# Forward borders of a linear-attention and GLU training step: new order with residuals on TensorE, and backward weights transposed by DMA

## The chip, the cores and the metric

The kernel runs on one core of a Trainium2 chip. The metric is device time in microseconds for one execution. The kernel before takes 1199.76 us (median of three runs, 1198.84 to 1200.74).

## The reference

Four residual layers are computed forward, attention, feed-forward, attention, feed-forward, and then the gradients of all inputs. S = 2048 rows, D = 512, F = 1376, 32 heads of 16. Cut to what matters:

```python
def attention(x, wqkv, wo):                 # linear attention, H = 32, Dh = 16
    q, k, v = split_heads(x @ wqkv)
    phi = lambda t: where(t > 0, t + 1, exp(t)) + 1e-6
    pq, pk = phi(q), phi(k)
    kv = einsum("bhsd,bhse->bhde", pk, v)
    z = einsum("bhsd->bhd", pk)
    num = einsum("bhqd,bhde->bhqe", pq, kv)
    den = einsum("bhqd,bhd->bhq", pq, z)[..., None] + 1e-6
    return merge_heads(num / den) @ wo

def feed_forward(x, w_gate, w_up, w_down):
    return (sigmoid(x @ w_gate) * (x @ w_up)) @ w_down

x = x + attention(layernorm(x), wqkv, wo)
x = x + feed_forward(layernorm(x), w_gate, w_up, w_down)
x = x + attention(layernorm(x), wqkv, wo)
x = x + feed_forward(layernorm(x), w_gate, w_up, w_down)
# outputs: x, and the gradients for grad_out of x, wqkv, wo, w_gate, w_up, w_down
```

Both attention layers share their weights, and so do both feed-forward layers. Inputs and outputs are bf16.

## The kernel before

The 2048 rows are cut into 16 row tiles of 128 (`NST`), D into four chunks of 128 (`NDC`), F into eleven (`NFC`, the last of 96). The residual stream stays in SBUF as f32 tiles `k.xs`. The forward part runs as `kq_fwd` (layer 0), `ab_fwd` (layer 1), `kq_fwd` (layer 2), `ab_fwd` (layer 3); what the gradients need is stored to DRAM tensors (`sv_...`) and read again in the backward part, which follows.

`kq_fwd` does attention as far as it can go without all rows. For each row tile it computes phi of k and q, and adds h^T phi(k) into four PSUM banks (`X_some`, L612); `z_sum` adds phi(k) up on GpSimd. After the loop comes the border to the feed-forward: the last terms of z (L735, L738), the last X matmuls and X copies (L748 to L750), `kv_ps` (L758), its block-diagonal part `kvbdT` (L760), M = kvbdT times wo in four matmuls and copies (L763 to L766), the queries of the last two row tiles (`late_q`), and MT, which only the backward part reads (L772 to L783).

A row tile of attention output then goes through the steps of `attn_fronts`: `prod` (phi(q) times z), `front1` (sum per head, `den`), `front2` (1/den, and `pqn`), `front3` (transpose of pqn, `pqnT`), `attn_mm` (four matmuls with M, L854), `attn_add` (residual added on VectorE from PSUM, L862, then LayerNorm statistics, L448). LayerNorm goes on with three GpSimd steps (L451 to L454), `apply` on ScalarE (L459) and `stage_T`, the transpose that gives hT (L494, copied by VectorE).

`ab_fwd` loops over the row tiles. `gu` makes gate and up matmuls for each of three slices of F, two sigmoids on ScalarE (L911, L913), hh on VectorE (L914) and ssd on GpSimd (L915). `transposes` makes hhT (L923, copied by ScalarE, L926). `finish` is the down-projection of the row tile before (L935) and its residual. Between them stand the attention steps of row tiles ahead: `attn_y(st + 2)`, `front1` to `front3` of `st + 3`, `apply(st + 2)`, `stage_T(st + 1)`. At a row tile's end ssd, hdd and hdl are stored. `ssd_t`, `hh_t` and `hhT` have two buffers each. The tables of ScalarE change with the functions: one line loads that for Sigmoid ahead of the feed-forward (L771).

Weights in transposed form, for the gradients, are made on TensorE: `wT_groups_a` (wqkv and wo, in layer 1) and `wT_groups_b` (w_down, w_up, w_gate, in layer 3) give groups of up to four 128x128 transposes in one PSUM bank with one evacuation. The class `Fill` hands them out in `A.tail` and at places in the loop of `ab_fwd`, `fill("t", ...)`, so that they are spread over the row tiles.

TensorE, ScalarE, VectorE and GpSimd run their instructions in the order in which the program issues them (`tc.manual_schedule`). The order on SP, which issues all DMAs, is set by the scheduler. PSUM is divided into pools by name: "t" two banks, "g" two, "u" two, "y" one, "ln" one.

Of the kernel before, what the change touches and what calls it, by code (L numbers as in the profile page):

```python
# [10 lines left out]
F32 = mybir.dt.float32  # L11
# [31 lines left out]


def pair_cols(fc):
    if fc == NFC - 1:
        return slice(fc * P, F)
    c0 = fc // 2 * 2 * P + fc % 2
    return slice(c0, c0 + 2 * P - 1, 2)
# [18 lines left out]
def kernel(  # L68
# [78 lines left out]
    with tc.tile_pool(name="wfwd", bufs=1, reuse_waits="tile") as wfwd, ExitStack() as lctx, tc.manual_schedule(engines=EM):  # L147
# [44 lines left out]
        with tc.tile_pool(name="aq0", bufs=1, reuse_waits="tile") as aq:  # L192
            A = kq_fwd(k, aq, 0, lns[0], lns[1], x_bf)
            with tc.tile_pool(name="wt_stage", bufs=2, reuse_waits="tile") as wt_stage:
                fill = Fill(wT_groups_a(k, wt_stage))
                A.tail(fill)
                ab_fwd(k, A, lns[1], fill, nxt=lns[2])
        xctx.close()
        with tc.tile_pool(name="aq2", bufs=1, reuse_waits="tile") as aq:
            A = kq_fwd(k, aq, 2, lns[2], lns[3])  # L200
            hctx.close()
            wb = bctx.enter_context(tc.tile_pool(name="wbwd", bufs=1, side="right", reuse_waits="tile"))
            ocur = {}
# [27 lines left out]
            fill = Fill(wT_groups_b(k, wb))  # L231
            A.tail(fill)
            ab_fwd(k, A, lns[3], fill, out_cb=out_cb, last_cb=last_cb)
# [5 lines left out]
    if True:  # L239
        def load_b_weights():  # L240
            k.wdT = wb.tile([P, NDC, F], BF16, name="wdT", tag="w_c")
            nc.sync.dma_start(out=k.wdT[:], in_=k.wT["wdT"].rearrange("(c p) f -> p c f", p=P))
            k.wuT = wb.tile([P, NFC, D], BF16, name="wuT", tag="w_a")
            k.wgT = wb.tile([P, NFC, D], BF16, name="wgT", tag="w_b")
            for t_sb, t_d in ((k.wuT, k.wT["wuT"]), (k.wgT, k.wT["wgT"])):
                nc.sync.dma_start(out=t_sb[:], in_=t_d.rearrange("(c p) j -> p c j", p=P))
# [130 lines left out]
def wT_groups_a(k, stage):  # L377
    nc = k.nc
    groups = []
    for w_sb, wT_d, C in ((k.wqkv, k.wT["wqkvT"], 3 * D), (k.wo, k.wT["woT"], D)):  # L380
        for cc0 in range(0, C // P, 4):
            holder = {}
            for j in range(4):
                def g(bank, w_sb=w_sb, wT_d=wT_d, cc0=cc0, j=j, holder=holder):
                    if j == 0:
                        holder["t"] = stage.tile([P, 4, D], BF16, name="wt_st")
                    cc = cc0 + j
                    ps = ps_tile(k, bank, [P, 8, P], BF16, "wT_ps")
                    for rc in range(NDC):
                        nc.tensor.transpose(ps[:, rc, :], w_sb[:, rc, cc * P:(cc + 1) * P], k.ident[:])  # L390

                    def ev(eng):
                        evac_copy(k, holder["t"][:, j, :], ps[:, 0:NDC, :].rearrange("p a b -> p (a b)"), eng)
                        if j == 3:
                            nc.sync.dma_start(
                                out=wT_d[cc0 * P:(cc0 + 4) * P, :].rearrange("(n p) d -> p n d", p=P),
                                in_=holder["t"][:])
                    return ev
                groups.append(g)
    return groups  # L400


def wT_groups_b(k, wb):
    nc = k.nc
    groups = []
    k.wdT = wb.tile([P, NDC, F], BF16, name="wdT", tag="w_c")
    k.wuT = wb.tile([P, NFC, D], BF16, name="wuT", tag="w_a")
    k.wgT = wb.tile([P, NFC, D], BF16, name="wgT", tag="w_b")
    for cc in range(NDC):
        for fs in range(3):  # L410
            def g(bank, cc=cc, fs=fs):
                fcs = fchunks_of_slice(fs)
                ps = ps_tile(k, bank, [P, 8, P], BF16, "wT_ps")
                for i, fc in enumerate(fcs):
                    r = fc_rows(fc)
                    nc.tensor.transpose(ps[:, i, 0:r], k.wd[0:r, fc, cc * P:(cc + 1) * P], k.ident[0:r, 0:r])
                c0, w = FSL[fs]

                def ev(eng):
                    evac_copy(k, k.wdT[:, cc, c0:c0 + w], ps[:].rearrange("p a b -> p (a b)")[:, 0:w], eng)  # L420
                    if cc == NDC - 1 and fs == 2:
                        nc.sync.dma_start(out=k.wT["wdT"].rearrange("(c p) f -> p c f", p=P), in_=k.wdT[:])
                return ev
            groups.append(g)
    for w_sb, wT_sb, wT_d in ((k.wu, k.wuT, k.wT["wuT"]), (k.wg, k.wgT, k.wT["wgT"])):
        for cc in range(NFC):
            def g(bank, w_sb=w_sb, wT_sb=wT_sb, wT_d=wT_d, cc=cc):
                r = fc_rows(cc)
                if cc == 0:
                    nc.gpsimd.memset(wT_sb[FLAST:P, NFC - 1, :], 0.0)  # L430
                ps = ps_tile(k, bank, [P, 8, P], BF16, "wT_ps")
                for rc in range(NDC):
                    nc.tensor.transpose(ps[0:r, rc, :], w_sb[:, rc, pair_cols(cc)], k.ident[:])

                def ev(eng):
                    evac_copy(k, wT_sb[0:r, cc, :], ps[0:r, 0:NDC, :].rearrange("p a b -> p (a b)"), eng)
                    if cc == NFC - 1:
                        nc.sync.dma_start(out=wT_d.rearrange("(c p) j -> p c j", p=P), in_=wT_sb[:])
                return ev
            groups.append(g)  # L440
    return groups
# [20 lines left out]
class FwdLN:  # L462
# [9 lines left out]
    def stats(self, st):  # L472
        if st < NST:
            self.nmr[st] = ln_stats(self.k, self.k.xs[st][:], self.rstd(st))
# [13 lines left out]
    def stage_T(self, st):  # L488
        if st >= NST:
            return  # L490
        k = self.k
        h_t = self.hs.pop(st)
        hT = k.lnres["hT"].tile([P, NDC, P], BF16, name="hT")
        transpose_blocks(k, k.ps["ln"], hT[:], [h_t[:, c * P:(c + 1) * P] for c in range(NDC)], "vector", tag="ln_tp")  # L494
        self.hTs[st] = hT
# [60 lines left out]
def kq_fwd(k, aq, l, ln, ln_next, x_src=None):  # L556
# [10 lines left out]
    with ExitStack() as ctx:  # L567
# [7 lines left out]
        else:  # L575
            X_sb = big.tile([P, NDC, D], BF16, name="X_sb")
            MT_sb = big.tile([P, NDC, D], BF16, name="MT_sb")
        cnt = [0]
# [155 lines left out]
        z_ps = mm_tile()  # L734
        nc.tensor.matmul(z_ps[:], lhsT=k.ones32[:], rhs=zs, start=True, stop=False)  # L735

        def z_mm(st):
            nc.tensor.matmul(z_ps[:], lhsT=k.ones_sq[:], rhs=pk_all[:, st, :], start=False, stop=(st == NST - 1))  # L738

        for st in range(NST - ZLAG, NST - 1):  # L740
            z_mm(st)
        X_some(NST, NST - 2)
        z_mm(NST - 1)
# [3 lines left out]
        A.front2(0)  # L747
        for ic in range(NDC):  # L748
            X_mm(NST - 1, ic)
            nc.scalar.copy(X_sb[:, ic, :], X_ps[ic][:])  # L750
        nc.sync.dma_start(out=sv["X"].rearrange("(c p) j -> p c j", p=P), in_=X_sb[:])

        kv_ps = ps_tile(k, "y", [P, D], F32, "kv_ps")
        kv3 = kv_ps[:].rearrange("p (c f) -> p c f", c=NDC)
        for c in range(NDC):
            cs = slice(c * P, (c + 1) * P)
            for ic in range(NDC):
# [1011 lines left out]
```

## Time and profile before

| what | value |
|---|---|
| runs | 1199.76 us median, 1198.84 to 1200.74 |
| profiled execution | 1199.19 us, span 1197.5 us, mean granted clock 0.998 |
| TensorE, VectorE, ScalarE, GpSimd busy | 1175.6, 730.5, 593.2, 290.2 us |
| layer 0 `kq_fwd` and border | to 53.6 us, to 79.8 us |
| layer 1 `ab_fwd` | 79.8 to 221 us |
| layer 2 `kq_fwd` and border | to 260.3 us, to 285.4 us |
| layer 3 `ab_fwd` | 285.4 to about 429 us |
| backward part | to the end |

The span is what lies between the first and the last instruction of the profiled execution; its time is 1.7 us longer. Times in the trace count from the span's start. A border is taken here from the end of the attention loop to the gate matmuls of the second row tile. Lines of the timeline name the instruction, its operands by the program's names, how many instructions are joined in the row, and in brackets the idle time before it with the engine and tile that ended it.

### The profile page before, as it was taken

To read this page: it belongs to the slowest core of one execution; us is meant where nothing else is said; L and a number is where in the kernel's file an instruction comes from. 1 tells how busy PE (TensorE), PEld (TensorE's weight loads), DVE (VectorE), ACT (ScalarE), POOL (GpSimd) and SP (SyncE) were. 2 spreads that over 40 slices of the span, in tenths; PEclk is the share of its full clock that TensorE was granted. 3 is DMA by queue.
4 is the path that set the end of the run, shared out by engine and by line. 5 is a ranking of instruction groups with operands and counts; after the bars stand their busy time and mean duration, and the time that the engine had idled before them with its cause. 6 is when DMAs were issued, how large, how long until landed. Compare 5 with 4: busy or idle time off the path is not lost.

```text
span 1197.5 us, 21853 instructions
## 1 busy us (share of the span) xinstructions
PE 1175.6 (98%) x8302; PEld 717.0 (60%) x8302; DVE 730.5 (61%) x1414; ACT 593.2 (50%) x1100; POOL 290.2 (24%) x498
## 2 busy tenths in 40 slices
PE   8989999998999999999999999999999999999999
PEld 4445555544555555555556568965556745547888
DVE  7788886777777556665784760056664976761211
ACT  6667776546776754543644651144444635630010
POOL 5646765425666410000110010000100110110000
PEclk9999999999999999999999999999999999999999
DMA  8834455434446777976856859558897685749875
GB/s 269 291 124 164 169 177 186 155 137 166 179 152 220 248 224 249 333 228 208 260 177 200 251 162 314 141 157 260 257 296 223 219 262 169 220 127 338 280 199 163
DMA packets 266233, 256.05 MB, mean 214 GB/s; under 512 B 43280, under 2 KB 251024, under 8 KB 261264
## 3 DMA queue, kind: packets, MB, share of 16 engines
q1 hardware_dynamic: 266128, 254.65, 66.6%
q8 instruction: 65, 1.06, 0.4%
q14 instruction: 40, 0.33, 0.1%
HBM read 135.69 MB, written 118.92 MB: 213 GB/s over the span
## 4 chain that ended last, share of the span: by engine, by line
PE 93%; DVE 4%; ACT 2%; DMA 1%; issue 0%; POOL 0%; DVEq 0%; ACTq 0%
PE p_ps L1412 17%; PE dh_ps L1174 13%; PE dh_ps L1627 7%; PE p_ps L1396 6%; PE dhh_ps L1059 6%; PE u_ps L909 6%; PE g_ps L909 6%; PE y_ps L935 6%; PE T_ps L1134 3%; PE y_ps L854 2%; PE GT_ps L1539 2%; PE dpk_ps L1658 2%; PE dp_ps L1514 2%; PE t_mm L604 2%; PE t_tp L923 2%; PE X_ps L612 2%
## 5 line engine op out<-in xcount | busy, mean ns | idle before, releaser
L1412 PE MATMUL p_ps<-p_set,p_a 128*128 128x256 bf16 (+1 forms) x2032 | 210.3, 264 | 0.4 <-DVE dw_stg L1386 0.4
L1412 PEld LDWEIGHTS <-p_a 128*128 128x128 bf16 x2048 | 186.0, 98 | 22.8 <-issue 0.5
L1067 DVE TENSOR_TENSOR dd<-dhh_ps,ssd 128x512 bf16<-128x512 f32 x144 | 82.5, 629 | 134.3 <-PE dhh_ps L1059 131.3
L1138 ACT COPY ddT<-T_ps 128x1024 bf16<-128x1024 bf16 (+1 forms) x96 | 83.0, 867 | 124.7 <-PE T_ps L1134 124.3
L1033 POOL TENSOR_SCALAR ab<-c 128x2 f32<-128x2 f32 x64 | 12.3, 191 | 435.7 <-DVE junk L1030 421.5
L915 POOL TENSOR_TENSOR ssd_t<-hh_t,oms 128x512 bf16<-128x512 bf16 (+1 forms) x96 | 101.6, 1064 | 55.5 <-ACT out_t L219 41.1
L1174 PEld LDWEIGHTS <-ddT 128*128 128x128 bf16 (+1 forms) x704 | 67.7, 98 | 69.3
L909 PEld LDWEIGHTS <-hT 128*128 128x128 bf16 x768 | 71.1, 98 | 56.6 <-DVE hT L362 1.0
L1386 DVE TENSOR_TENSOR dw_stg<-p_ps,dw_stg 128x512 bf16<-128x512 f32 (+3 forms) x43 | 28.0, 653 | 106.7 <-PE p_ps L1412 84.9
L909 PE MATMUL g_ps<-wg,hT 128*128 128x512 bf16 (+1 forms) x384 | 90.0, 357 | 0.6 <-DVE hT L362 0.6
L909 PE MATMUL u_ps<-wu,hT 128*128 128x512 bf16 (+1 forms) x384 | 90.0, 357 | 0.0
L914 DVE TENSOR_TENSOR hh_t<-u_ps,ssd_t 128x512 bf16<-128x512 f32 (+1 forms) x96 | 61.0, 636 | 45.9 <-PE u_ps L909 24.5
L1174 PE MATMUL dh_ps<-wgT,ddT 128*128 128x512 bf16 (+1 forms) x352 | 86.2, 379 | 0.0
L1059 PE MATMUL dhh_ps<-wdT,gT 128*128 128x512 bf16 x372 | 82.5, 357 | 0.0
L935 PE MATMUL y_ps<-wd,hhT 128*128 128x512 bf16 (+1 forms) x352 | 81.3, 379 | 0.6 <-DVE x L937 0.6
L1174 PE MATMUL dh_ps<-wuT,ddT 128*128 128x512 bf16 (+1 forms) x352 | 81.3, 379 | 0.0
L1396 PE MATMUL p_ps<-p_a,p_set 128*128 128x512 bf16 (+1 forms) x352 | 81.2, 379 | 0.0
L1025 ACT ACTIVATE t_sb<-dh_ps,rstd_all 128x512 f32<-128x512 f32 x64 | 44.0, 687 | 72.1 <-issue 38.4
L1030 DVE SCALAR_TENSOR_TENSOR junk<-t_sb,h_ld 128x512 bf16<-128x512 f32 x64 | 44.0, 687 | 49.3 <-ACT t_sb L1025 48.4
L911 ACT ACTIVATE ssd_t<-g_ps 128x512 bf16<-128x512 f32 (+1 forms) x96 | 53.2, 554 | 30.8 <-PE g_ps L909 30.6
L1388 ACT CAST dw_stg<-p_ps 128x512 bf16<-128x512 f32 (+2 forms) x43 | 24.1, 560 | 65.9 <-PE p_ps L1412 58.9
L1396 PEld LDWEIGHTS <-p_set 128*128 128x128 bf16 (+1 forms) x352 | 33.6, 100 | 34.9
(241 smaller groups left out, 2164.4 us busy)
## 6 DMA issues: line engine op xcount, KB each, us to landing
p_set<-sv_hdd SPq DMA_DIRECT2D x30, 1024.0 KB, 6.0
sv_ssd<-ssd_t SPq DMA_DIRECT2D x32, 688.0 KB, 3.4
ssd<-sv_ssd SPq DMA_DIRECT2D x24, 688.0 KB, 5.1
sv_hdd<-dd SPq DMA_DIRECT2D x48, 320.0 KB, 3.6
sv_hdd<-hh_t SPq DMA_DIRECT2D x32, 320.0 KB, 2.6
h_ld<-sv_h SPq DMA_DIRECT2D x32, 256.0 KB, 4.6
p_a<-sv_h SPq DMA_DIRECT2D x16, 512.0 KB, 6.1
p_set<-sv_dqk SPq DMA_DIRECT2D x8, 1024.0 KB, 7.8
```

What stands on the lines that cost most here:

```text
L909: nc.tensor.matmul(ps[:, 0:w], lhsT=hT[:, kc, :], rhs=w_sb[:, kc, c0:c0 + w], start=(kc == 0), stop=(kc == NDC - 1))
L911: nc.scalar.activation(ssd_t[:, 0, c0:c0 + w], g_ps[:, 0:w], ACT.Sigmoid)
L914: nc.vector.tensor_tensor(hh_t[:, c0:c0 + w], u_ps[:, 0:w], ssd_t[:, 0, c0:c0 + w], ALU.mult)
L915: nc.gpsimd.tensor_tensor(ssd_t[:, 1, c0:c0 + w], hh_t[:, c0:c0 + w], oms[:, 0:w], ALU.mult)
L935: nc.tensor.matmul(y_ps[:], lhsT=T["hhT"][0:r, fc, :], rhs=k.wd[0:r, fc, :], start=(fc == 0), stop=(fc == NFC - 1))
L1059: k.nc.tensor.matmul(ps[:, 0:w], lhsT=gT[:, jc, :], rhs=k.wdT[:, jc, c0:c0 + w], start=(jc == 0), stop=(jc == NDC - 1))
L1067: k.nc.vector.tensor_tensor(dd[:, a, c0:c0 + w], ps[:, 0:w], ssd[:, a, c0:c0 + w], ALU.mult)
L1138: nc.scalar.copy(ddT[:, :, f0:f0 + nfull, :], tps[:, :, 0:nfull, :])
L1174: nc.tensor.matmul(T["dh"][:], lhsT=ddT_block(T, a, fc), rhs=(k.wuT, k.wgT)[a][0:r, fc, :], start=(i == 0), stop=(i == 2 * NFC - 1))
L1396: nc.tensor.matmul(ps[0:r, :], lhsT=set_t[:, st, c * P:c * P + r], rhs=self.ops[j["l"], "g"][:, st, :], start=(st == 0), stop=(st == NST - 1))
L1412: nc.tensor.matmul(ps[:, icl * w:(icl + 1) * w], lhsT=self.ops[j["l"], "h"][:, st, ic * P:(ic + 1) * P], rhs=set_t[:, st, 0:w], start=(st ...
L1627: nc.tensor.matmul(dh_ps[:], lhsT=lhsT, rhs=rhs, start=(i == 0), stop=(i == len(ops) - 1))
```

## The change

The transposes of weights on TensorE, their evacuations, `Fill` and `A.tail` are removed. In their place `wT_units` makes 13 units, given out one per row tile at row tiles 1 to 13 of layer 1: a DMA that transposes from an input in DRAM to the SBUF tile `wt_st` (two buffers), and a DMA that stores it in the transposed form to DRAM. Where w_up and w_gate have 352 columns left, a second transposing DMA takes the last 128, and the store takes 96 of them. The transposed w_down, w_up and w_gate are then loaded from DRAM in layer 3 (`b_weight_loads`), as they are for layer 1's gradients; the interleaving of rows that the transposes did with `pair_cols` is now done by these loads.

The border is reordered in both layers. z goes to the "y" bank ahead of the last X matmuls; the fourth X copy is on VectorE; the kv matmuls run with ic outermost; matmuls whose result nobody reads stand in between (`keep_on`); row tiles 0 and 1 have their residual added by a matmul with an identity into the PSUM bank of the attention output (`attn_res`), LayerNorm statistics read that bank directly, and ScalarE copies it to `k.xs` (`attn_out`); the Sigmoid table is loaded last. In `ab_fwd`, `attn_y(2)` and the steps of row tile 3 move to the end of row tile 0, `front3(3)` and `attn_y(3)` move later in row tile 1.

The diff, cut to its core:

```diff
+        if l == 0:
+            eye = k.ident
+        else:
+            eye = big.tile([P, P], F32, name="eye32")
...
+        def keep_on():
+            ps = ps_tile(k, "ln", [P, D], F32, "on_ps")
+            return lambda n: [nc.tensor.matmul(ps[:], lhsT=k.ident[:], rhs=pk_all[:, 0, :], start=True, stop=True)
+                              for _ in range(n)]
...
         A.front1(0)
-        A.front2(0)
+        X_some(NST, NST - 2)
         for ic in range(NDC):
             X_mm(NST - 1, ic)
-            nc.scalar.copy(X_sb[:, ic, :], X_ps[ic][:])
+            evac_copy(k, X_sb[:, ic, :], X_ps[ic][:], "vector" if ic == NDC - 1 else "scalar")
...
+        A.rden(0)
+        on = keep_on()
...
+        nc.vector.tensor_tensor(kvbdT[:], kv3, k.bdmask[:].unsqueeze(1).to_broadcast([P, NDC, P]), ALU.mult)
+        A.front2(0, False)
+        A.attn_res(0, eye)
+        if l == 0:
+            on(2)
...
+            evac_copy(k, A.M_sb[:, c, :], m_ps[c][:], "scalar" if c < 2 else "vector")
         A.front3(0)
+        phis = [late_q(NST - 2)]
+        A.attn_mm(0)
         A.prod(1, nc.vector)
+        A.attn_out(0)
+        A.prod(2)
         A.front1(1)
-        A.attn_y(0)
         A.front2(1)
-        phis = [late_q(st) for st in range(NST - QLATE, NST)]
-        nc.scalar.activation(k.tab[:], k.neg[:], ACT.Sigmoid)
...
+        mt_copy(0)
+        mt_copy(1)
+        phis.append(late_q(NST - 1))
+        A.ln.apply(0)
+        A.attn_res(1, eye)
+        if l == 0:
+            keep_on()(3)
+        A.front3(1, "vector")
+        mt_copy(2)
+        A.ln.stage_T(0, "scalar")
         phis[0]()
+        A.attn_mm(1)
+        mt_copy(3)
         nc.sync.dma_start(out=sv["MT"].rearrange("(c p) j -> p c j", p=P), in_=MT_sb[:])
-        A.attn_mm(1)
+        A.attn_out(1)
         phis[1]()
+        nc.scalar.activation(k.tab[:], k.neg[:], ACT.Sigmoid)
...
+    def attn_out(st):
+        y_ps = F_.pop(st)["y"]
+        A.ln.stats(st, y_ps[:])
+        nc.scalar.copy(k.xs[st][:], y_ps[:])
...
+def wT_units(k, stage, A_wqkv, A_wo, B_w_gate, B_w_up, B_w_down):
+    def by_rows(src, c0, n, dst):
+        def unit():
+            t = stage.tile([P, NDC, D], BF16, name="wt_st")
+            nfull = min(n, F // P - c0) if src.shape[-1] == F else n
+            nc.sync.dma_start(out=t[:, 0:nfull, :], in_=src[:, c0 * P:(c0 + nfull) * P], transpose=True)
+            if nfull < n:
+                nc.sync.dma_start(out=t[:, nfull, :], in_=src[:, F - P:F], transpose=True)
+            nc.sync.dma_start(out=dst[c0 * P:(c0 + nfull) * P, :].rearrange("(n p) d -> p n d", p=P),
+                              in_=t[:, 0:nfull, :])
...
+    def by_cols(src, f0, w, dst):
+        def unit():
+            t = stage.tile([P, NDC, D], BF16, name="wt_st")
+            v = t[:].rearrange("p a b -> p (a b)")[:, 0:NDC * w].rearrange("p (a b) -> p a b", a=NDC)
+            nc.sync.dma_start(out=v, in_=src[f0:f0 + w, :], transpose=True)
+            nc.sync.dma_start(out=dst.rearrange("(c p) f -> p c f", p=P)[:, :, f0:f0 + w], in_=v)
...
+            A.prod(st + FLAG)
             if st == 0:
+                A.front1(2)
                 gu(T, hT, 0)
-                A.extra("vector")
-                A.front1(FLAG)
-                A.front3(2)
+                A.front2(2)
                 ln.apply(1)
                 gu(T, hT, 1)
                 transposes(T, 0)
-                A.attn_y(2)
                 ln.stage_T(1)
                 gu(T, hT, 2)
-                A.front2(FLAG)
+                A.front3(2)
...
             transposes(T, 1)
+            if st == 0:
+                A.attn_y(2)
+                A.front1(FLAG)
+                A.front2(FLAG)
             ln.apply(st + YLAG)
...
-            if st > 0 and nfill > 1:
-                fill("t" * (nfill - 1), "scalar" if st % 2 else "vector")
             transposes(T, 2)
...
+            if st in side:
+                side[st]()
```

## The prediction

> **What bounds the kernel now.** I read the page's busy times and chain first, then busy time by stage (one window for each border and each feed-forward stage), the timeline of TensorE in the border, the rows of the removed transposes, the waits of SP and the DMA landings.
>
> ```profile
> PE 1175.6 (98%) x8302; PEld 717.0 (60%) x8302; DVE 730.5 (61%) x1414; ACT 593.2 (50%) x1100; POOL 290.2 (24%) x498
> q1 hardware_dynamic: 266128, 254.65, 66.6%
> PE 93%; DVE 4%; ACT 2%; DMA 1%; issue 0%; POOL 0%; DVEq 0%; ACTq 0%
> ```
>
> TensorE is the bound almost everywhere: 93% of the chain is its own work, so a matmul taken out of a stream that never pauses should be worth its whole length. The 6% of the chain on DVE and ACT must sit in the places where it does pause, which the windows show (columns: length, busy PE, PEld, DVE, ACT, POOL, granted clock, DMA share, GB/s):
>
> ```profile
> 53.60:79.80 26.20, 20.57 (x141) 10.83 (x140) 20.64 (x44) 15.33 (x28) 7.58 (x12) 0.93 0.32 111
> 79.80:200.00 120.20, 119.69 (x799) 64.99 (x798) 100.18 (x189) 87.17 (x170) 80.96 (x128) 1.00 0.50 174
> 260.30:285.40 25.10, 19.43 (x140) 10.35 (x139) 19.93 (x43) 15.23 (x28) 7.58 (x12) 1.00 0.27 95
> 285.40:416.00 130.60, 130.18 (x909) 73.09 (x907) 93.12 (x179) 91.11 (x187) 77.90 (x97) 1.00 0.59 203
> ```
>
> Rows 2 and 4 are the two feed-forward stages: TensorE idles 0.5 and 0.4 us in them, while DVE, ACT and POOL have 17% or more to spare. Rows 1 and 3 are the borders, with 5.6 and 5.7 us of idle TensorE each. In the first the granted clock is 0.93: two windows of 2 us from 59.60 and 61.60 show 0.56 and 0.59, and 1.00 stands on both sides. The border's own timeline (start, length, idle before and its releaser):
>
> ```profile
> 60.20 1.89 PE L765 MATMUL M_ps<-wo,kvbdT 128*128 128x512 bf16 x4 [0.56 <-DVE kvbdT L760]
> ...
> 67.99 1.04 PE L854 MATMUL y_ps<-M_sb,pqnT 128*128 128x512 bf16 x4 [1.03 <-ACT pqnT L364]
> ...
> 70.49 1.04 PE L909 MATMUL g_ps<-wg,hT 128*128 128x512 bf16 x4 [0.28 <-DVE hT L362]
> ...
> 73.94 0.40 PE L355 MATMUL ln_tp<-ident,pqnstage 128*128 128x128 bf16 x4 [1.54 <-DVE pqnstage L833]
> ```
>
> Four matmuls of M_ps took 1.89 us where four of the same size take 1.04 at 67.99. The pauses are handovers of DVE and ACT, the longest while the first row tile of the feed-forward is already running.
>
> **Transposes off TensorE: the gain.** 196 transposes go. Their price is read inside a stream, as the distance to the next start:
>
> ```profile
> 201.30 0.39 PE L390 MATMUL wT_ps<-ident,wo 128*128 128x128 bf16 x4
> 201.52 1.03 PE L909 MATMUL g_ps<-wg,hT 128*128 128x512 bf16 x4
> ```
>
> Four cost 0.22 us, 0.0555 each. In layer 1, 16 of the 64 stand in the border and 48 later: 48 x 0.0555 = 2.66 us. In layer 3, 22 of the 132 stand before the third row tile's gate matmuls (295.49) and 110 later: 6.10 us. Together 8.8 us of full stream. The 38 early ones fall into stretches that wait for DVE, so I count them with the borders. Of cover: a row tile without a transpose already runs in 8.95 us (down-projections at 95.70 and 104.65) against 9.2 with four and 9.4 with two groups, so no other engine holds the tile at its old length. The 50 evacuations that leave DVE and ACT (0.38 to 0.59 us each) are worth nothing, since neither engine bounds a stage.
>
> **Transposes to the DMA queue: the risk.** 13 units go to SP, one per row tile from 1 to 13 of layer 1, most of them one transposing DMA of 512 KB from the input to wt_st and one store of it. The tile wt_st has two buffers, so a transpose waits for the store two units back, and a store waits at the head of SP for its transpose. SP's order in the changed program is: transpose, then ssd, hdd, hdl (and pqn or h) of a row tile, then the unit's store. Queued behind a waiting store are the next tile's ssd and hh stores; for these wait the sigmoids and products two row tiles on, as ssd_t and hh_t have two buffers each. SP has room: between 100 and 200 us it waits 74 us for engines, nearly all with nothing to do. The rows for the wait and for landings:
>
> ```profile
> SPq L1006 <- DVE hh_t L914: 44.3, 10, 7.1
> wqkvT_d<-wt_st SPq DMA_DIRECT2D x3, 512.0 KB, 2.9
> p_a<-sv_h SPq DMA_DIRECT2D x16, 512.0 KB, 6.1
> p_set<-sv_hdl SPq DMA_DIRECT2D x6, 384.0 KB, 4.3
> ```
>
> Issues are cheap (0.36 to 0.50 us in the timeline, two or three per unit: at most 1.5 us of the 6.8 that SP has free per tile). What no trace of before shows is a transposing DMA. Lower bound: 4.3 us, the p_set row, which reads 2048 runs of 192 B as a unit reads 2048 of 256 B; the plain load of the same size takes 6.1. Upper bound, an estimate: if each run is written as eight pieces, 16384 pieces at the p_set row's rate above the shortest landing (4.3 - 1.6 us over 2048, 1.3 ns each), some 23 us. Up to about 9 us (a row tile) the wait lies beside other stores and costs nothing; above, each unit costs the excess. I take 6 us, the nearest row by bytes and source, so 0; both ends stay for the range. The DMA share of row 2 rises from 0.50 to about 0.75 (6.3 MB more read and 4.2 MB more stored in 120 us, 87 GB/s beside 174), still free.
>
> The page "VectorE: DVE Perf Modes" of the Trainium skill, section "The three transpose paths", speaks against the change: it gives 1309 ns for a 128x128 transpose by DMA and 390 ns on TensorE. Sixteen blocks one after another would be an estimated 21 us per unit, and the sum by it 13 x 12 us = 156 us more, 1346 us; the trace already differs on TensorE's side (0.0555 us in a stream). The page "Advanced Engine Details and Errata", section "X-Bar Transpose (TRN2)", says that transposing DMAs are as fast as plain ones, by which the sum stays as it is; no run so far shows either.
>
> In layer 3 the stores of wdT, wuT and wgT (4.2 MB) leave and loads of as much come. They stand on SP at the layer 2 border, where the share is 0.27, and take 6.0 to 6.9 us each in the rows of the same tiles. The store of MT is queued behind them, and the first ACT copy into hhT, which takes MT's memory, waits for that store: 0 to 1.5 us, I take 0.5. The same loads for layer 1's backward have 62 us of weight-gradient matmuls over them: 0.
>
> **Borders, layer 0.** I laid the new order out by hand with the durations of before (ACT casts 0.59, DVE on PSUM 0.69, reduce 0.68, POOL's three LayerNorm steps 1.06 from start to end, matmuls 0.216 at 512 columns). z before the last X costs a wait of about 0.5 us for pk_all and lets the den chain start earlier; the fourth X copy on DVE ends the X copies 0.5 us sooner; the residual matmul (0.216) takes the DVE addition (0.69) off the path to the statistics; seven dummy matmuls (1.5 us) lie in pauses. The first gate matmul comes at 67.6 where it was 70.49, the second row tile's at 75.7 where it was 79.80. Then the gain is given back. The residual of row tile 2 is now computed at the end of tile 0 (y at 74.7), its LayerNorm apply sits on ACT in front of the copy hhT and the sigmoids of tile 1, and TensorE pauses 1.8, 1.0 and 0.7 us there. The third tile's gate matmuls come at 88.5 where they were 89.52: 1.0 us. The copy of x on ACT also waits for the statistics, which read the same PSUM bank; behind it on ACT stand MT's copies, the table load (1.28 us, now last) and the first sigmoids: up to 0.6 us back. I take 0.7, with 0 to 1.2 for the range. The 1.0 holds if the clock stays full; the pauses of tile 1 come to 3.5 us, and a half clock for as long as before (1.7 us lost on eight matmuls) would turn it into a loss of 0.7 to 1.3.
>
> **Borders, layer 2.** There the clock was 1.00 before, so nothing of it is to win; the residual is an f32 matmul (1.02 us for two in the y_mm row of L735, so 0.86 in four passes). The same walk puts the third tile's gate matmuls at 294.64 against 295.49: 0.1 to 0.8, I take 0.4.
>
> Sum against the profiled execution's own 1199.19 us: 8.8 + 0.7 + 0.4 - 0.5 = 9.4, so **1189.8 us**; the median of the runs, 1199.76, is 0.6 above that execution, within their spread.
>
> **Rivals.** *SP paces layer 1.* If a transpose takes more than a row tile (about 9 us), each of 13 units holds SP, and with it ssd and hh, by the excess: at 10 us 13 more, at 12 us 39, at 23 us 182; on top of 1189.8 that is 1203, 1229 and 1372. It decides against the change from 9.7 us on. For it: the rows of before hold no such DMA, and SP is one queue in order with the stores that the row tile needs. Against: all rows of this size lie at 2.9 to 8.1 us. Chance 0.34. *The borders cost.* Half clock in both tile-1 pauses (2 x 1.7) and the full MT wait (1.0 more) and x copies (1.0 more): 5.4 of the 9.4 gone, 1195 us; the clock rows at 59.60 speak for it, the 1.00 in layer 2 with pauses as long (1.54, 1.07) against. Chance 0.10. *Nothing comes out of the removed transposes*, because the row tile is held by DVE's 100.18 of 120.20 us and its order: about 1198.5 us. The 8.95 us tile speaks against. Chance 0.03.
>
> **How the numbers follow.** The forecast has 0.53; its own range is 1187 to 1193.5 (borders 0.6 to 1.5 us better or worse, the MT wait, one half-clocked border). The range for all cases is 1186 to 1229: above it lies the upper half of the first rival (0.16), below it a few per cent in which the borders keep their early lead. A measurement of this kernel tells about 0.2%, 2.4 us. Faster by more: 0.53 and most of the border case (its 1195 is 4.6 below the median), 0.60. Same: the rest of that case, 0.03, the third rival, 0.03, and 0.01 of the first. Slower: the rest of the first, 0.33.
>
> **What would show it.** Right: no wT_ps rows, row tiles of 8.95 us in both feed-forward stages, wt_st rows that land in 4 to 8 us, SP waits without wt_st on the chain, third gate matmuls near 88.5 and 294 to 295 (less in layer 2 what the earlier stages gained), first border at a clock of 1.00. Wrong: wt_st landings over 9 us, ACT or DVE waiting for SP's stores of ssd_t or hh_t, a first feed-forward stage longer than 141 us, windows at 0.5 to 0.6 of the clock in tile 1.

## The result and the profile after

The changed kernel takes 1194.56 us (median of six runs, 1192.51 to 1197.01) against 1200.05 before (median of six runs): ratio 0.9955, 95% interval 0.9942 to 0.9968. It is faster, by 5.5 us where 9.4 were forecast. The profiled execution is the fastest of the six, 1192.51 us, so the traces differ by 6.7 us (spans 1197.5 and 1190.8).

The page of the changed kernel, busy times, DMA queue and chain:

```profile
PE 1168.3 (98%) x8121; PEld 707.5 (59%) x8121; DVE 716.5 (60%) x1370; ACT 589.9 (50%) x1094; POOL 290.7 (24%) x498
...
q1 hardware_dynamic: 296032, 265.14, 71.4%
...
PE 89%; DVE 5%; DMA 2%; ACT 2%; issue 1%; POOL 0%; SPq 0%; DVEq 0%; POOLq 0%
```

TensorE's share of the chain fell from 93 to 89%: the kernel now waits more, and DMA's share of the chain rose from 1 to 2%. The same windows as before (length, busy PE, PEld, DVE, ACT, POOL, granted clock, DMA share, GB/s):

```profile
53.60:79.80 26.20, 22.91 (x147) 11.36 (x146) 19.44 (x41) 15.61 (x29) 8.90 (x14) 1.00 0.68 207
79.80:200.00 120.20, 116.21 (x747) 61.64 (x745) 97.67 (x178) 86.80 (x172) 80.00 (x127) 1.00 0.86 248
260.30:285.40 25.10, 22.35 (x144) 11.22 (x142) 18.48 (x39) 15.82 (x30) 9.21 (x15) 1.00 0.93 303
285.40:416.00 130.60, 127.71 (x830) 69.60 (x829) 88.15 (x161) 93.30 (x192) 78.13 (x96) 1.00 0.53 184
```

The borders hold less idle TensorE than before (3.3 and 2.8 us, part of what is busy there being the matmuls that nobody reads), but the feed-forward stages, full before, now idle 4.0 and 2.9 us. The mean DMA share of 0.86 in the second row hides a change inside it: in windows of 10 us from 70 to 160 us the share is 0.93 to 1.13, so the DMA engines are busy nearly all the time there, and from 170 to 190 us it is about 0.4. Fixed windows cut different work in the two kernels, so I use marks of the program instead: z of each attention layer, the gate matmuls of the third row tile, and the last down-projection of layer 3. Lengths in us between the marks, from the timelines of the profiled executions:

| stage | before | changed | old borders, DMA transposes | later apply | later apply, early 1/den |
|---|---|---|---|---|---|
| start to z, layer 0 | 53.57 | 53.57 | 54.11 | 53.91 | 53.83 |
| border, layer 0 | 35.95 | 36.02 | 34.25 | 34.40 | 34.38 |
| layer 1 to z of layer 2 | 170.74 | 169.83 | 170.57 | 170.59 | 169.02 |
| border, layer 2 | 35.23 | 35.46 | 34.19 | 33.82 | 33.81 |
| layer 3 | 130.96 | 124.62 | 124.63 | 124.62 | 124.62 |
| rest | 771.05 | 771.30 | 771.15 | 771.46 | 771.34 |

Layer 3 gave 6.34, layer 1 gave 0.91, and the new borders gave nothing (0.07 and 0.23 lost). Where their early lead went is in row tile 1 of the feed-forward (TensorE, and one row of ScalarE):

```profile
67.70 1.03 PE L894 MATMUL g_ps<-wg,hT 128*128 128x512 bf16 x4
...
76.86 1.03 PE L894 MATMUL g_ps<-wg,hT 128*128 128x512 bf16 x4
...
82.41 0.40 PE L908 MATMUL t_tp<-ident,hh_t 128*128 128x128 bf16 x4 [1.52 <-DVE hh_t L899]
83.60 0.38 PE L355 MATMUL ln_tp<-ident,hstage 128*128 128x128 bf16 x4 [0.80 <-ACT pqnT L364]
...
86.82 2.54 PE L920 MATMUL y_ps<-wd,hhT 128*128 128x512 bf16 x11 [0.56 <-DVE x L865]
...
89.59 1.03 PE L894 MATMUL g_ps<-wg,hT 128*128 128x512 bf16 x4
```

```profile
79.90 0.81 ACT L428 ACTIVATE hstage<-x,ln_nmr,rstd_all 128x512 bf16<-128x512 f32 x1 [3.65 <-POOL ln_nmr L423]
```

The first gate matmuls come 2.8 us earlier than before (67.70 against 70.49), the third row tile's do not (89.59 against 89.52). ScalarE stood for 3.65 us before the LayerNorm apply of row tile 2, with the sigmoids of row tile 1 behind it. My theory after this reading was that this one wait takes the borders' gain, and that in layer 1 VectorE's chain to pqnstage takes the gain of the removed transposes. The rivals were that the DMAs or SP take both, and that the clock does.

### The profile page after: what moved, and what is told of

Read it like the earlier page. It is cut to its first block, busy times and chain, and to the rows that moved or that the text cites. A ratio compares the mean times of both kernels' runs of the same rounds, so it can differ in the third digit from the quotient of the medians.

```text
span 1190.8 us, 21442 instructions
## 1 busy us (share of the span) xinstructions
PE 1168.3 (98%) x8121; PEld 707.5 (59%) x8121; DVE 716.5 (60%) x1370; ACT 589.9 (50%) x1094; POOL 290.7 (24%) x498
## 4 chain that ended last, share of the span: by engine, by line
PE 89%; DVE 5%; DMA 2%; ACT 2%; issue 1%; POOL 0%; SPq 0%; DVEq 0%; POOLq 0%
PE p_ps L1394 17%; PE dh_ps L1156 13%; PE dh_ps L1609 7%; PE p_ps L1378 6%; PE dhh_ps L1041 6%; PE y_ps L920 5%; PE u_ps L894 5%; PE g_ps L894 5%; PE T_ps L1116 3%; PE GT_ps L1521 2%; PE dp_ps L1496 2%; PE dpk_ps L1640 2%; PE t_mm L580 2%; PE y_ps L857 2%; PE X_ps L588 2%; PE t_tp L908 1%
## 5 line engine op out<-in xcount | busy, mean ns | idle before, releaser
L920 PEld LDWEIGHTS <-hhT 128*128 128x128 bf16 (+1 forms) x352 | 33.2, 98 | 36.3 <-issue 2.1
```

Source lines behind the costliest of these rows:

```text
L920: nc.tensor.matmul(y_ps[:], lhsT=T["hhT"][0:r, fc, :], rhs=k.wd[0:r, fc, :], start=(fc == 0), stop=(fc == NFC - 1))
```

## The experiments

Times are medians; the kernel before ran beside each group at 1199.2 to 1200.2 us.

**One part alone.** The kernel before with the transposes by DMA and its borders as they were, and the new borders with the transposes on TensorE:

```diff
 # old borders, DMA transposes (on the kernel before)
-                fill = Fill(wT_groups_a(k, wt_stage))
-                A.tail(fill)
-                ab_fwd(k, A, lns[1], fill, nxt=lns[2])
+                units = wT_units(k, wt_stage, A_wqkv, A_wo, B_w_gate, B_w_up, B_w_down)
+                A.tail(Fill([]))
+                ab_fwd(k, A, lns[1], {st + 1: u for st, u in enumerate(units)}, nxt=lns[2])
...
 # new borders, transposes on TensorE (on the changed kernel)
+            nfill = fill.share(st)
...
                 after(st - 2)
+                if nfill > 0:
+                    fill("t", "vector")
                 gu(T, hT, 1)
...
+            if st > 0 and nfill > 1:
+                fill("t" * (nfill - 1), "scalar" if st % 2 else "vector")
```

> The borders of before, with the transposes by DMA and without those on TensorE. Theory (the borders give nothing, all of the gain is the transposes): as fast as the changed kernel's best, 1192 to 1193 us in the profiled execution, with the clock of before (0.998) and runs as close together as before's (within 2 us). Rival (the new borders hold part of the gain): 1195 to 1197 us.

> The new borders alone, with the transposes on TensorE inside the loop of the feed-forward. Theory: the borders give nothing, and 38 transposes more lie in full stream (2.1 us, of which up to 0.8 us hide in the pauses of row tile 1), so 1200 to 1201.5 us, with runs that spread over 4 us as those of the changed kernel do. Rival (the borders gain, and the DMAs took it away again): 1196 to 1198 us.

Old borders with DMA transposes: 1190.95 us (1190.53 to 1193.40; ratio to before 0.9929, 0.9916 to 0.9941). New borders alone: 1206.71 (1204.07 to 1207.32; 1.0054, 1.0041 to 1.0066). The first went beyond either expectation: not only do the new borders give nothing, the change is 3.6 us slower with them than without. Taking the 38 transposes out of the old borders shortened these by 1.7 and 1.0 us (34.25 and 34.19 in the table), part of the 1.7 being a half clock that stood at this place only in the profile of before. So those transposes had not been free, although they stood in stretches that wait; the new order has shed them too and is still no shorter than the old one with them. The second run missed both of its expectations as well: it is some 5 us above its theory. In its trace (1204.07) layer 3 is 2.7 us longer than before and the borders 0.7 and 1.0 us, one wait there being a pause of 2.21 us of TensorE for ScalarE's copy hhT, ahead of a group of transposes in row tile 1. What makes up the rest stays open.

**Transposing DMAs left out, and doubled.**

```diff
 # left out: stores of one zeroed tile stay
+    zero = stage.tile([P, NDC, D], BF16, name="wt_zero")
+    nc.gpsimd.memset(zero[:], 0.0)
...
-            t = stage.tile([P, NDC, D], BF16, name="wt_st")
+            t = zero
-            nc.sync.dma_start(out=t[:, 0:nfull, :], in_=src[:, c0 * P:(c0 + nfull) * P], transpose=True)
...
 # doubled: each of them
+            nc.sync.dma_start(out=t[:, 0:nfull, :], in_=src[:, c0 * P:(c0 + nfull) * P], transpose=True)
             nc.sync.dma_start(out=t[:, 0:nfull, :], in_=src[:, c0 * P:(c0 + nfull) * P], transpose=True)
```

> The changed kernel without the transposing DMAs: the stores stay and write a tile of zeros, so the gradients that use these weights are left out in effect, with every instruction still there. Theory (the 9.25 us of every second row tile in layer 1 comes from VectorE's own chain to pqnstage, the transposing DMAs are hidden): within 0.5 us of the changed kernel's profiled 1192.5, and still every second row tile at 9.25. Rival (DMA traffic or waits on SP stretch these row tiles): all row tiles at 8.95 and 1.8 us less, 1190.7.

> The changed kernel with every transposing DMA issued twice in a row into the same tile, so a unit takes about 4.5 us more and SP carries 15 more issues of 1.3 to 3.5 us. Theory (the queue was near its limit: SP issued without a gap from 115 to 165 us of the changed kernel and cost 0.6 us there): the slower rival of the prediction becomes real, each unit holds SP 3 to 4 us beyond a row tile, 20 to 45 us more, 1213 to 1238 us. Rival (SP has a third of a row tile free, all of it stays hidden): not over 3 us more, 1194 to 1197.

Left out: 1194.91 us (1194.49 to 1197.93), as the changed kernel. Layer 1 took 169.58 us against 169.83, and every second row tile still 9.26 (for instance down-projections at 115.46 and 124.72). So the transposing DMAs cost 0.25 us in the changed kernel's trace, and the 9.25 us is not theirs. Doubled: 1204.44 (1203.18 to 1206.80; 1.0042, 1.0029 to 1.0055). Layer 1 took 178.22 us, 8.4 more; the row tiles grow to 11.11 and 13.84 us at 162 to 187 us, where hh waits for stores that stand in SP's queue (1.7 us of the longer one are a half clock from 182 to 188 us, behind the wait). The two rows of the waits between 160 and 190 us that name a DMA (total, times, longest):

```profile
DVE hh_t L902 <- DMA sv_hdl<-hh_t: 9.1, 2, 5.3
...
ACT ssd_t L899 <- DMA sv_ssd<-ssd_t: 3.9, 1, 3.9
```

That lies between both expectations: a margin exists, and 15 more such DMAs use it up. The forecast's slower rival was a real mechanism, one factor of two away. Whether SP's issues or the DMA engines themselves set this limit was not separated: the share is at 0.96 to 1.19 in this kernel from 100 to 200 us.

**The apply of row tile 2 later.**

```diff
-            ln.apply(st + YLAG)
+            if st > 0:
+                ln.apply(st + YLAG)
...
                 gu(T, hT, 1)
                 if st == 1:
+                    ln.apply(YLAG)
                     A.front3(FLAG)
```

> The changed kernel with one step moved: the LayerNorm apply of row tile 2 goes from the end of row tile 0, where ScalarE waited 3.65 us for it, to row tile 1, behind the sigmoids of its second slice. Theory (this wait at the head of ScalarE is where the borders' early lead went): TensorE's pauses of 1.52 and 0.80 us in row tile 1 shrink, the third row tile's gate matmuls come 1.5 to 2.1 us earlier in each layer, and the time is 3 to 4 us less: about 1189 in the profiled execution, 1190.5 median. Rival (VectorE's and GpSimd's chain from y of row tile 2 holds row tile 1 anyway): not over 0.5 us less.

1190.52 us (1189.76 to 1191.93; 0.9923, 0.9909 to 0.9936), 4.0 less than the changed kernel. Both borders shrink by 1.6 us (36.02 to 34.40, 35.46 to 33.82), as the theory said. Row tile 1 of this kernel on TensorE:

```profile
81.45 0.40 PE L908 MATMUL t_tp<-ident,hh_t 128*128 128x128 bf16 x4 [0.21 <-DVE hh_t L899]
82.32 0.38 PE L355 MATMUL ln_tp<-ident,hstage 128*128 128x128 bf16 x4 [0.47 <-ACT pqnT L364]
```

The pause of 1.52 is 0.21, that of 0.80 is 0.47. The wait at the head of ScalarE is shown to be the place. Its price is smaller than the 4.0: the traces, 1192.51 and 1190.52 us, differ by 2.0, as the borders give 3.3 and layer 1 takes 0.8 back in two long row tiles (below). The rest of the 4.0 is scatter: the changed kernel's median lies 2.05 us above its profiled execution, this kernel's is its profiled execution.

**VectorE's chain in layer 1.** The row tiles of layer 1 alternate between 8.95 and 9.25 us. VectorE of the changed kernel in a long one, whose down-projection starts at 95.77 and whose transposes of pqnstage start at 98.44, 0.29 us after it could end (95.77 + 11 x 0.216), and GpSimd beside it:

```profile
95.82 0.52 DVE L899 TENSOR_TENSOR hh_t<-u_ps,ssd_t 128x352 bf16<-128x352 f32 x1
96.26 0.81 DVE L811 TENSOR_SCALAR den<-den 128x32 f32<-128x32 f32 x1
97.11 0.35 DVE L812 RECIPROCAL rden_all<-den 128x32 f32<-128x32 f32 x1
97.49 0.90 DVE L823 TENSOR_TENSOR pqnstage<-pq_all,rden_all 128x512 bf16<-128x512 bf16 x1
...
95.88 1.96 POOL L900 TENSOR_TENSOR ssd_t<-hh_t,oms 128x512 bf16<-128x512 bf16 x2
```

The last row joins two products of GpSimd, of 1.15 and 0.85 us. The den step of 0.81 us ends at 97.07, just when the first product does (97.03). In the next, short row tile the product starts earlier against it (104.84), den (at 105.52) takes 0.52 us and again ends with the product. The difference of 0.29 us is that between the two row tiles.

First I took the copy of hT from VectorE, alone and with the later apply:

```diff
-                ln.stage_T(st + 1)
+                ln.stage_T(st + 1, "scalar" if l == 1 and st > 1 else "vector")
```

> The changed kernel with the copy of hT on ScalarE instead of VectorE, from row tile 2 of layer 1 on. Theory (VectorE's row of work up to pqnstage ends last in every second row tile there): the row tiles of 9.25 us fall to 8.95 to 9.05, 1 to 2 us less, 1191 in the profiled execution. Rival (the 0.3 us belongs to another wait, ScalarE's or SP's): no row tile shorter, 1192.5 or more.

> The later apply of row tile 2 together with the copy of hT on ScalarE in layer 1. Theory: both gains add, 1188.5 to 1189.5 us median, faster than the kernel with the old borders (1190.95) and than the one with the later apply alone (1190.52). Rival: the copy brings nothing, 1190.5.

It brought nothing: 1195.29 us (1193.06 to 1197.83) alone, 1190.38 (1189.89 to 1193.21) with the later apply. The row tiles still alternate (161.50, 170.75, 179.70). VectorE has less to do, but hh of the third slice now waits 0.36 us for the sigmoid that stands on ScalarE behind the copy. What had to be shortened was the chain after hh, not VectorE's load:

```diff
                 A.front1(st + FLAG)
+                if st + FLAG < NST:
+                    A.rden(st + FLAG)
                 gu(T, hT, 2)
...
-                A.front2(st + FLAG)
+                A.front2(st + FLAG, False)
```

> The changed kernel with the two short steps of 1/den on VectorE moved ahead of the third slice of each row tile, so that between hh of that slice and pqnstage nothing is left. Theory (the 9.25 us of every second row tile of layer 1 is the chain hh, den (0.5 to 0.8 us beside GpSimd's ssd product instead of 0.17), 1/den, pqnstage (0.90), which ends 0.25 us after the down-projection): all row tiles of layer 1 at 8.95, 1.5 to 1.8 us less in layer 1, 169.8 to 168.2 us from the third gate matmuls to z of layer 2. Rival (another wait has this length): row tiles as before.

> The later apply of row tile 2 and the early 1/den together. Theory: both gains add to 5 to 6 us below the changed kernel, 1188.5 to 1189.5 us median, the fastest so far. Rival (the wait is not in this chain): 1190.5 as with the later apply alone.

> The old borders with DMA transposes and the early 1/den. Theory: 1.5 us below the 1190.95 of the old borders, 1189 to 1190; with the run before, on the same chip, it tells what the new border is worth once its wait is gone: 0.3 to 0.8 us less for the new one. Rival: the old borders are as fast or faster.

With 1/den ahead of the slice, the row tiles between 88.50 and 133.24 us are all of 8.95 (97.44, 106.39, 115.34, 124.29), and from 161.61 on again. The chain, in the kernel with this edit alone:

```profile
97.50 0.18 DVE L811 TENSOR_SCALAR den<-den 128x32 f32<-128x32 f32 x1
97.71 0.35 DVE L812 RECIPROCAL rden_all<-den 128x32 f32<-128x32 f32 x1
97.98 0.46 DVE L899 TENSOR_TENSOR hh_t<-u_ps,ssd_t 128x352 bf16<-128x352 f32 x1
98.36 0.88 DVE L823 TENSOR_TENSOR pqnstage<-pq_all,rden_all 128x512 bf16<-128x512 bf16 x1
```

So the chain is shown as the cause of the 9.25. Layer 1 fell to 169.18 us, not to 168.2: two row tiles, from 133.24 to 152.66, took 9.82 and 9.60. Alone, the edit gave 1196.01 us (1193.01 to 1198.01), no gain to be measured beside the scatter of a kernel that still has the pause of row tile 1. With the later apply it gave the fastest kernel of all, **1189.10 us** (1188.67 to 1191.05; 0.9915, 0.9901 to 0.9928). On the old borders it gave 1190.34 (1189.16 to 1191.66). That is 1.2 us more by the medians, but the runs overlap, and the borders themselves are not longer: 33.85 and 33.77 us against 34.38 and 33.81. So the new order shortens neither border even without its wait, as the rival of that expectation said. In the traces, which differ by 0.5 us, the new kernel gains 1.0 in layer 1 (170.01 against 169.02) and loses 0.5 in the first border. In layer 1 the row tiles of the old-border kernel are 9.1 us, not 8.95, up to 148.62: its early den step falls almost wholly beside GpSimd's product and takes 1.04 to 1.08 us. That the border's order sets how the two engines meet there was not tested.

**The two long row tiles near 140 us.** The kernels with the later apply, with the early 1/den and with the old borders have two row tiles of 9.6 to 10.0 us there; the changed kernel has one, of 9.54 (141.46 to 151.00). Its program gives out one unit per row tile, but SP's order runs ahead of that: the last transpose is issued before 151 us, in the ninth of the 16 row tiles. SP issues almost without a gap there; its rows of the 12th and 13th unit and the next store (start, time of the issue), and a window with the DMA share as its last number but one:

```profile
143.91 6.62 SPq L385 DMA_TRANSPOSE wt_st<-in_A_wqkv_dram  x2
150.58 0.57 SPq L985 DMA_DIRECT2D sv_ssd<-ssd_t  x1
...
140.00:150.00 10.00, 9.59 (x65) 5.10 (x63) 8.59 (x17) 7.28 (x15) 6.93 (x13) 1.00 1.13 288
```

The waits from 130 to 152 us name the stores that stood behind such rows:

```profile
DVE hh_t L899 <- DMA sv_hdl<-hh_t: 1.9, 1, 1.9
...
ACT ssd_t L896 <- DMA sv_ssd<-ssd_t: 1.1, 1, 1.1
```

The last experiment bound each unit to the end of its own row tile, on top of the later apply and the early 1/den:

```diff
-                ab_fwd(k, A, lns[1], {st + 1: u for st, u in enumerate(units)}, nxt=lns[2])
+                ab_fwd(k, A, lns[1], dict(zip((1, 2, 3, 4, 5, 6, 8, 9, 10, 12, 13, 14, 15), units)), nxt=lns[2])
...
-            nc.sync.dma_start(out=sv["hdl"][0, :, st, :], in_=T["hh"][:, NG * GW:F])
+            last = nc.sync.dma_start(out=sv["hdl"][0, :, st, :], in_=T["hh"][:, NG * GW:F])
             if st in side:
-                side[st]()
+                if l == 1:
+                    with tc.issue_after(last.ins):
+                        side[st]()
```

> The later apply of row tile 2, the early 1/den, and the 13 units bound to SP's place behind the hdl store of their own row tile, with one row tile left free after each of the two units that have two transposes and two stores. Theory (the two row tiles of 9.6 to 9.7 us near 130 to 150 us come from a backlog on SP: several units' transposes and stores in a row, with ssd and hdl behind them): these row tiles fall to 8.95, 1.3 us less than with the two edits alone, 187.5 us or so in place of 188.7 above 1000, that is 1187.5 in the profiled execution. Rival (the transposes slow other DMAs wherever they stand, or a store that waits for its transpose at the head of SP now delays pqn and h): other row tiles grow instead, 1188.7 or more.

1195.51 us (1193.26 to 1195.65): slower, though all row tiles of layer 1 were 8.95 (from 86.13 to 193.51 in 12 of them). So the units in a row were the cause of the long row tiles; whether by SP's queue or by the load on the DMA engines is open, as spreading them relieved both (a share of 0.71 from 140 to 150 us instead of 1.08). But the last transpose now stands after the end of layer 1, and the start of layer 2 pays: its first rows of TensorE are

```profile
218.47 1.03 PE L580 MATMUL u_mm<-wqkv,hT 128*128 128x512 bf16 x4
224.35 3.57 PE L580 MATMUL t_mm<-wqkv,hTst 128*128 128x512 bf16 x8 [4.85 <-DVE pk_all L603]
```

a pause of 4.85 us and a half clock behind it (eight matmuls in 3.57 us instead of 1.89). In that kernel's chain the time before this is the transpose (4.20 us of DMA wt_st) and 3.97 us of issue, in which the profile shows no wait; what fills these is open. A version with the units spread and ended a row tile or two earlier was not tried.

**The clock.** Six profiles have the pause of row tile 1. Four of them show a stretch of half clock right behind it: those without the transposing DMAs, with the doubled ones (both layers), with hT on ScalarE and with the early 1/den alone. Those of the changed kernel and of the new borders alone (where the pause is 2.21 us in layer 1) do not. Two-microsecond windows of the kernel without transposing DMAs:

```profile
82.00:84.00 2.00, 0.77 (x8) 0.66 (x9) 1.06 (x2) 2.00 (x5) 1.50 (x2) 0.80 1.01 343
84.00:86.00 2.00, 2.00 (x9) 1.03 (x8) 1.02 (x2) 0.64 (x3) 0.77 (x1) 0.50 0.78 276
86.00:88.00 2.00, 1.74 (x10) 0.85 (x9) 0.97 (x2) 0.46 (x2) 0.67 (x1) 0.84 0.00 0
```

It cost 1.7 us (0.20 + 0.50 + 0.16 of 2 us each), which at half speed is an estimated 3.4 us; this kernel's border is 37.33 us instead of 36.02. No profile of a kernel without the pause has it in row tile 1. To see whether this makes the changed kernel's scatter I filled the pause:

```diff
                 if st == 1:
                     A.front3(FLAG)
+                    ps = ps_tile(k, "y", [P, D], F32, "on_ps")
+                    for _ in range(7):
+                        nc.tensor.matmul(ps[:], lhsT=k.ident[:], rhs=k.wd[:, 0, :], start=True, stop=True)
```

> The changed kernel with seven matmuls whose result nobody reads (1.5 us) in the pause of row tile 1, ahead of its first transposes of hh, in both layers. Theory (its runs lie up to 4.5 us above the fastest because the clock drops to half after this pause in some of them): every run at a clock of 1.000, all within 1.5 us, median 1192.5 to 1193.5 us instead of 1194.56. Rival (the spread has another cause): median and spread as before the dummies, clocks of 0.997 to 0.999 in half of the runs.

1196.11 us (1193.89 to 1197.50): median and spread did not improve, so the expectation failed. Its profiled execution (1197.50) has the borders of the changed kernel (36.04 and 35.48) at full clock, but starts 1.46 us later (z at 55.03) and loses 3.6 us after layer 3: one output store took 7.97 us to land, TensorE waited 2.50 us for its buffer near 1160 us, and half a clock followed there too. So times move at three places at least, the loading at the start, that store, and half clocks behind pauses; how much of the changed kernel's 4.5 us is each stays open, as its five other runs have no trace.

## Why the prediction was right or wrong

The direction held, and so did the range for all cases, 1186 to 1229, which is wide because it had to hold the rival of slow DMAs. The forecast itself was 4.8 us too low: the median lies outside its own range of 1187 to 1193.5. It was worked out for one profiled execution, and there (1192.51) it missed by 2.7 us; the other 2.1 are the scatter of the changed kernel's runs above the fastest, for which it had no term. By its steps, in the traces:

- **Layer 3's transposes, 6.10 us:** measured 6.34, all row tiles at 8.95. Right in mechanism and size.
- **Layer 1's transposes, 2.66 us:** measured 0.91. This is the mis-sized term. "No other engine holds the tile at its old length" rested on one row tile of before without transposes (95.70 to 104.65). The trace of before held the sign against it: the row tile ahead of that one (86.20 to 95.70) has no transpose either and took 9.50, with a pause for pqnstage,

```profile
89.12 0.40 PE L355 MATMUL ln_tp<-ident,pqnstage 128*128 128x128 bf16 x4 [0.38 <-DVE pqnstage L833]
```

  and without transposes the old borders' row tiles run 9.49, 8.95, 9.26, 8.96 from 85.05 us on. In the changed kernel's long row tiles VectorE's chain from hh to pqnstage, slowed beside GpSimd's product, ends 0.25 to 0.3 us after the down-projection could. With four transposes in the row tile, before, this wait was under 0.1 us and den took 0.50 to 0.58, so a long row tile took 9.25 there as well: what the transposes left, the wait took. So only the groups in the short row tiles, which went from 9.17 to 8.95, were worth their length, about half of the 2.66. Layer 3 shows nothing of it: there the den step takes 0.24 us, because GpSimd's product has nearly ended when it starts (310.50). That the next layer's statistics, which only layer 1 adds, make this difference is argued from the rows, not tested.
- **Transposing DMAs, 0:** measured 0.25 in the changed kernel (inside layer 1's figure), 1.0 to 1.5 in others with the same units (two row tiles near 140 us). They land in 4.4 to 5.8 us by the medians of their sources, 7.0 at most (6 forecast), but occupy SP for 1.3 to 3.8 us at each issue where 0.36 to 0.50 was assumed. The share rose to 0.86 over the window (0.75 forecast, "still free") and to about 1 while the units ran. One of the forecast's signs of being wrong did show, for a short time: VectorE and ScalarE waited 1.9 and 1.1 us for SP's stores of hh_t and ssd_t. The landings, with a plain load of 512 KB in the same trace:

```profile
wt_st<-in_B_w_up_dram SPq DMA_TRANSPOSE x4, 4.4
...
wt_st<-in_A_wo_dram SPq DMA_TRANSPOSE x1, 5.8
...
p_a<-sv_h SPq DMA_DIRECT2D x16, 512.0 KB, 5.8
```

  The rule of the Trainium skill's page "Advanced Engine Details and Errata", section "X-Bar Transpose (TRN2)", that transposing DMAs are as fast as plain ones, agrees with these rows. The 1309 ns that the Trainium skill's page "VectorE: DVE Perf Modes", section "The three transpose paths", gives for one 128x128 block cannot be added up: a unit of 16 blocks took 4.5 to 7.0 us, not 21.
- **Borders, +0.7 and +0.4:** measured -0.07 and -0.23. The order was walked rightly up to the first gate matmuls (67.6 forecast, 67.70). The pauses of row tile 1 were named with their cause (1.8, 1.0 and 0.7 forecast; 1.52, 0.80 and 0.56 measured), but the third gate matmuls came at 89.59 instead of 88.5: 1.2 us was already gone at the second row tile (76.86 instead of 75.7). Half of that is pqnstage, which took 1.32 instead of the usual 0.69 (at 72.45, beside GpSimd's product). The 38 early transposes, "counted with the borders" as nothing, don't enter this difference, since both the walk and the measurement compare with the borders of before, which had them. But counting them so hid that their removal alone is worth 1.7 and 1.0 us, and that the new order takes this back.
- **MT's store, -0.5:** nothing. The first copy into hhT behind the layer 2 border starts 1.25 us after its transposes, as in layer 0, where no store of weights stands ahead.
- The rival "the borders cost", 1195 us, came closest to the measured 1194.56, but by luck. Its sum was another one: the changed kernel's trace has neither the MT wait nor a half clock, and what was lost instead is layer 1's chain, the borders' wait at the head of ScalarE and the scatter.

## What to carry to other kernels

Work that fills a pause can still cost its length, and work in a full stream can cost less than its length where another engine's chain has the same stretch as its own: look at every kind of row tile, also at the one next to the tile that has no filler. When a step is moved later, follow it to the instruction that waits for it on an in-order engine, and move that instruction too; here one apply on ScalarE was worth 3.3 us of the two borders. And price a DMA by what it occupies on its issuing queue and by the DMA engines' share in short windows, as well as by its landing: here nearly all of it stayed hidden, and twice as many such DMAs did not.

## What the runs showed of the hardware

- The den step on VectorE (128x32) takes 0.18 us alone and 0.24 to 1.08 us while GpSimd runs its bf16 product, by how much of the product is left: in the rows above it ends within 0.05 us of the product's end. The pqnstage product takes 0.69 alone and 0.88 to 1.32 beside it. The reciprocal of the same 128x32 takes 0.35 in both cases. The Trainium skill's page "SBUF — State Buffer", section "SBUF: two separate sides", names the cause, a port pair that VectorE and GpSimd share and that one instruction holds for its whole length; the trace agrees with a hold to the end of GpSimd's product, but no run here separates the port from other causes.
- The issue of a transposing DMA occupies SP for 1.3 to 3.8 us, that of a plain store with nothing ahead 0.33 to 0.5. The first two, issued at 69.58 and 72.09, took 2.05 and 2.12, before any backlog; the longest stood where the DMA share was about 1.
- Half clock came for an estimated 3.4 us, behind two pauses of 1.52 and 0.80 us, in four profiles of six with such pauses. It also came behind pauses of 2.50 and 4.85 us. The Trainium skill's page "TensorE: Matmul & The Clock Gate", Part 1, gives 3.4 us as the window of the gate; the length agrees, but the pauses of row tile 1 were shorter than it. With the transposes of 128x128 between and around them they come near it: in the kernel without transposing DMAs TensorE ran nothing else from 80.51 to 84.00 us. Whether transposes count as work for the clock was not tested.
